# A one-core FFT and GEGLU kernel: the opening's gathers, first weights and early transforms put in another order, and later folds moved by some slots

## The chip, the cores and the metric

The kernel runs on one core of one Trainium2 chip. The metric is device microseconds of one execution. Each run below was timed beside runs of the kernel before on the same chip. The profiled span is about 1.8 us shorter than the time of the same execution, so spans are compared with spans and times with times.

The engines have the names of the profile: PE is TensorE (PEld its weight loads), DVE is VectorE, ACT is ScalarE, POOL is GpSimd, and SP is SyncE, whose queue issues transfers. An eviction is the copy by ACT or DVE of a matmul's result from a `ps_` tile to the tile where it is used.

## The reference

```python
def _attn_ref(x):                     # x: (8, 3008, 256) float32
    X = np.fft.fft(x, axis=1)
    X = np.fft.fft(X, axis=2)
    return X.real.astype(np.float32)

def _moe_ref(x, w_gate, w_val, w_out):   # 24064 tokens, d 256, d_ff 1536
    g = x @ w_gate
    gelu = 0.5 * g * (1.0 + erf(g * inv_sqrt2))
    val = x @ w_val
    return (gelu * val @ w_out).astype(np.float32)
```

The real part of a two-dimensional Fourier transform of each of eight batches goes through a gated feed-forward layer.

## The kernel before

The kernel splits each sequence into an even part E and an odd part O, by adding and subtracting x and its mirror image. The mirror comes by an indirect transfer with an index (a gather, issued by POOL). For one batch the steps are: fold (x and mirror to `eo_sb`), stage 1 (matmuls with `G`), an identity transform (`ch`, to `Z_sb`), twiddle transforms (`tp_e`, `tp_o`, `tp_y`, to `EO_sb` and `EB_sb`), and then the feed. The feed has 36 slots for each batch, 288 in all. A slot has the gate matmuls, two gelus on ACT (0.59 us each), the value matmuls, three DVE operations (0.66, 0.60 and 0.60 us from one start to the next), one product on POOL (1.15 us) and, from slot 12 on, two second-layer pieces of four matmuls (0.85 us together). `plan()` puts everything else into slots: transforms and loads as "fill", folds as "pool". The first transforms of batch 0 come before the feed, in `opening()`; all the others run hidden beside it.

The end of the opening:

```python
    def opening():
        # ... staging loads, constants, gathers, weight loads (see the diff)
        warm(9)                       # dummy matmuls; the number is how many
        vec_fills(); vec_consts(); g_phases()
        g_sin(9, 7); g_sin_ends(); g_sin(1, 8)
        t_columns()                   # ten tiny matmuls: "parity columns", L371
        t_phases(); t_sin()
        warm(15)
        cw_phases(); cw_sin()
        # ... gelu_table() is the load of ACT's gelu table, L395
        # ... folds and stage 1 of batch 0, piece by piece
        stage1(0)
        ch(0, 0)()
        ch(0, 1, "V")()               # "V": DVE evicts, otherwise ACT
        make_w(0, 0, 256, engine="V")()
        tp_e(0, 0)()
        tp_o(0, 0, "V")()
        make_w(1, 0, 256, engine="V")()
        tp_y(0, 0)()
        make_yw(0, 256)()
```

The parts of the plan that the change touches, and the load and the row copies:

```python
        for i, f in enumerate(early):          # batch 0, groups 1 and 2: ch, ch, tp_e, tp_o, tp_y
            at(fill, (3, 4, 5, 6, 6, 7, 8, 10, 11, 12)[i], f)
        # ...
        def spread(b, items, s0, s1):
            each = len(items) // NG
            for i, f in enumerate(items):
                s = s0 + i * (s1 - s0) // (len(items) - 1)
                at(fill, s, f)
                if i % each == each - 1:
                    at(fill, s + 1, tp_rows(b, i // each))
        # ...
        for b in range(2, B):
            s0 = (b - 1) * NS
            # ... ops: the folds of batch b
            first, n = (s0 - 13, 29) if b == 2 else (s0 - 22, 32)
            slot_of = [first + i * n // len(ops) for i in range(len(ops))]
            # ... folds into pool; loads of the batch after:
                    at(fill, slot_of[piece * per + 1] + 1, lambda b=b, k=k: load_part(b + 1, k))
            s = s0 - 9
            for i, (jg, piece) in enumerate(((2, 1), (1, 2), (0, 3), (3, 4))):
                ready = slot_of[piece * per + per - 1] + 1
                for g in range(2):
                    s = max(s + 1, ready)
                    at(fill, s, s1t(b, jg, g))
            # ... z_write, z_read, and the transforms by spread(b, items, s + 7, ...)

    def load_part(b, k):
        j0, nj = ((9, 8), (1, 8), (0, 1))[k]
        load_forward(b, j0, nj)       # plain load, SP's queue, L152
        load_mirror(b, j0, nj)        # gather, POOL's queue, L158

    def tp_rows(b, gi):               # one row of Z's transform, from DRAM
        def run():
            # 128 copies of the row to EB_sb (128 KB), L588, then once to EO_sb (1 KB), L590;
            # both on SP's queue
            nc.sync.dma_start(out=_sub(EB_bufs[b], ...), in_=...)
            nc.sync.dma_start(out=_sub(EO_bufs[b], ...), in_=...)
        return run
```

Of the kernel before, what the change touches and what calls it, by code (L numbers as in the profile page):

```python
# [28 lines left out]
def kernel(  # L29
# [69 lines left out]
    def stage_tile():  # L99
        return work([NPX, 9, C], FP32, "h", 2, "x_stage")  # L100
# [247 lines left out]
    def cw_sin():  # L348
        nc.scalar.activation(_sub(CW, [[256, 2], [1, 128]], 0), cd[:, :], AF.Sin, scale=-TWO_PI)
# [380 lines left out]
    def opening():  # L730
        stage[0] = stage_tile()
        xb[0] = xb_tile(0)
        for j0, nj, at in ((9, 8, 0), (0, 1, 8)):
            nc.sync.dma_start(
                out=_sub(stage[0], [[1, nj * C]], at * C),
                in_=ap_replace(x, ap=[[32 * C, NPX], [1, nj * C]], offset=x.offset + j0 * C))
        pool_consts()
        index_consts(0)
        cast_mirror(0, 9, 8)
        pool_consts2()  # L740
        index_consts(1)
        cast_mirror(0, 0, 1)
        cast_forward(0, 1, 8)
        cast_mirror(0, 5, 4)
        cast_mirror(0, 1, 4)
        for f0, n in ((0, 256), (256, 256), (512, 1024)):
            load_w(f0, n)
        for q in range(4):
            load_wo(q)
        idle = gelu_tile()[:, 0, :]  # L750
        nc.vector.memset(idle, 0.0)

        def warm(n):

            ps = psum("o")
            for _ in range(n):
                nc.tensor.matmul(ps[:, :], idle[:, 0:128], idle[:, :], start=True, stop=True)  # L757

        def fold_piece(j0, nj):
            for f in fold_ops(0, j0, nj, nc.vector):  # L760
                f()

        def stage1(jg):
            s1(0, jg, 0)()
            s1(0, jg, 1, "V" if jg == 0 else "A")()

        warm(9)
        vec_fills()
        vec_consts()
        g_phases()  # L770
        g_sin(9, 7)
        g_sin_ends()
        g_sin(1, 8)
        t_columns()
        t_phases()
        t_sin()
        warm(15)
        cw_phases()
        cw_sin()
        nc.vector.tensor_scalar(keep2, col_p, 1.0, None, op0=ALU.min)  # L780
        nc.vector.tensor_scalar(keep2, keep2, -2.0, None, op0=ALU.mult)
        gelu_table()
        t_write()
        identities()
        cw_rest()
        fold_piece(9, 4)
        stage1(2)
        warm(4)
        fold_piece(13, 4)
        fold_piece(0, 1)  # L790
        stage1(3)
        warm(5)
        fold_piece(5, 4)
        stage1(1)
        warm(3)
        fold_piece(3, 2)
        fold_piece(1, 2)
        stage1(0)
        ch(0, 0)()
        ch(0, 1, "V")()  # L800
        make_w(0, 0, 256, engine="V")()
        tp_e(0, 0)()
        tp_o(0, 0, "V")()
        make_w(1, 0, 256, engine="V")()
        tp_y(0, 0)()
        make_yw(0, 256)()

    NS = NG * NFC

    def plan():  # L810

        fill, pool = {}, {}

        def at(table, s, f):
            table.setdefault(s, []).append(f)

        early = []
        for gi in (1, 2):
            early += [ch(0, 2 * gi), ch(0, 2 * gi + 1, "V"), tp_e(0, gi), tp_o(0, gi, "V"), tp_y(0, gi)]
        for s, f in (  # L820
                (0, make_w(0, 256, 256)), (0, make_w(1, 256, 256)), (1, make_yw(256, 256)),
                (1, make_w(1, 512, 512, (1,))), (2, make_w(0, 512, 512, (0,))), (2, make_yw(512, 512)),
                (3, make_w(0, 512, 512, (1,))), (3, make_w(1, 512, 512, (0,))),
                (4, make_w(1, 1024, 512, (1,))), (5, make_w(0, 1024, 512, (0,))), (5, make_yw(1024, 512)),
                (6, make_w(0, 1024, 512, (1,))), (7, make_w(1, 1024, 512, (0,)))):
            at(fill, s, f)
        for i, f in enumerate(early):
            at(fill, (3, 4, 5, 6, 6, 7, 8, 10, 11, 12)[i], f)

        def second_x():  # L830
            xb[1] = xb_tile(1)
            cast_forward(1, 9, 8)

        for s, f in (
                (0, second_x), (1, lambda: cast_mirror(1, 9, 8)), (2, lambda: cast_forward(1, 0, 9)),
                (3, lambda: cast_mirror(1, 5, 4)), (4, lambda: cast_mirror(1, 1, 4)),
                (5, lambda: cast_mirror(1, 0, 1))):
            at(fill, s, f)
        ops = []
        for piece in PIECES:  # L840
            ops += fold_ops(1, *piece, nc.gpsimd)
        slot_of = [6 + i * 13 // len(ops) for i in range(len(ops))]
        for s, f in zip(slot_of, ops):
            at(pool, s, f)
        s = 10
        for jg, piece in ((2, 1), (1, 2), (0, 3), (3, 4)):
            for g in range(2):
                s = max(s + 1, slot_of[2 * piece + 1] + 1)
                at(fill, s, s1(1, jg, g))
        last1 = s  # L850
        for k, s in ((0, 18), (1, 19), (2, 19)):
            at(fill, s, lambda k=k: load_part(2, k))
# [10 lines that stand above are left out]
        items = []  # L863
        for gi in range(NG):
            items += [ch(1, 2 * gi), ch(1, 2 * gi + 1), tp_y(1, gi), tp_e(1, gi), tp_o(1, gi)]
        spread(1, items, last1 + 1, NS - 3)
        for b in range(2, B):
            s0 = (b - 1) * NS
            ops = []
            for j0, nj in PIECES:  # L870
                ops += fold_ops(b, j0, nj, nc.gpsimd)
            per = len(ops) // 5
            first, n = (s0 - 13, 29) if b == 2 else (s0 - 22, 32)
            slot_of = [first + i * n // len(ops) for i in range(len(ops))]
            for s, f in zip(slot_of, ops):
                at(pool, s, f)
            if b + 1 < B:
                for k, piece in ((0, 1), (1, 3), (2, 4)):
                    at(fill, slot_of[piece * per + 1] + 1, lambda b=b, k=k: load_part(b + 1, k))
            s = s0 - 9  # L880
            for i, (jg, piece) in enumerate(((2, 1), (1, 2), (0, 3), (3, 4))):
                ready = slot_of[piece * per + per - 1] + 1
                for g in range(2):
                    s = max(s + 1, ready)
                    at(fill, s, s1t(b, jg, g))
                if i == 2:
                    at(fill, s + 1, z_write(b, 0, 12))
                if i == 3:
                    at(fill, s + 1, z_write(b, 12, 4))
            at(fill, s + 3, z_read(b))  # L890
            items = []
            for gi in range(NG):
                items += [tp_y(b, gi), tp_e(b, gi), tp_o(b, gi)]
            assert s + 7 < s0 + NS - 10
            spread(b, items, s + 7, s0 + NS - 3)
        return fill, pool

    def feed():
        blocks, works = [], []
        for b in range(B):  # L900
            for parts, l2s in ffn_work(b):
                works.append(l2s)
                blocks += [(parts, fc) for fc in range(NFC)]
        fill, pool = plan()
        pend, before = [], None
        for i, (parts, fc) in enumerate(blocks):
            if fc == 0 and i:
                assert not pend
                pend = list(works[i // NFC - 1])
            parts["G"][fc]()  # L910
            if before:
                before[0]["g"][before[1]]()
            parts["V"][fc]()
            if pend:
                pend.pop(0)()
            for f in pool.pop(i, []):
                f()
            if before:
                before[0]["v"][before[1]]()
            if pend:  # L920
                pend.pop(0)()
            for f in fill.pop(i, []):
                f()
            before = parts, fc
        assert not fill and not pool
        before[0]["g"][before[1]]()
        before[0]["v"][before[1]]()
        for u in works[-1]:
            u()
# [33 lines left out]
```

## Time and profile before

| | before |
|---|---|
| time, median of 3 runs | 635.71 us (635.58 to 636.37) |
| profiled span | 633.9 us |
| TensorE busy | 620.3 us, 98% |
| first gate matmul starts | 22.70 us |
| first gelu of slot 0, of slot 12 | 23.35 us, 49.38 us |

The busy times of the engines, from the page of before (busy us, share of the span, number of instructions):

```profile
PE 620.3 (98%) x4289; PEld 409.6 (65%) x4289; DVE 582.4 (92%) x937; ACT 433.0 (68%) x855; POOL 505.8 (80%) x511
```

TensorE is close to full, but that is an average. The view of waits of before, for TensorE from 60 us to the end, has what TensorE waited for, then us in total, times, and the longest:

```profile
PE ps_dft L508 <- POOL eo_sb L224: 1.2, 1, 1.2
PE ps_o L695 <- POOL h_sb L671: 0.3, 1, 0.3
PE ps_dft L695 <- POOL h_sb L671: 0.3, 1, 0.3
```

So after 60 us only 1.8 us of waiting is left, 1.2 of it in one place, stage 1 of a batch that waits for POOL's fold. The chain of waits of before (start, us, what) puts that place at 124 us:

```profile
123.16 1.28 POOL eo_sb L224
```

Everything else that can be won is in the opening and in the slots without second-layer work. From the timeline of before (start us, us, engine, line, operation, count; in brackets the idle time before it and what ended that):

```profile
3.44 1.56 POOL L281 IOTA par<- 1x128 f32 x1
3.67 1.36 DVE L322 TENSOR_SCALAR ff<-ff 94x24 f32<-94x24 f32 x1
5.27 2.29 PE L371 MATMUL ps_v<-one,par 1*128 1x1 f32 x10
7.49 6.02 PE L757 MATMUL ps_o<-gelu_sb 128*128 128x512 bf16 x15
11.20 1.28 ACT L395 ACT_TABLE_LOAD   x1
15.38 0.47 ACT L473 ACTIVATE A_sb<-ps_g 128x384 bf16<-128x384 f32 x1
22.70 0.61 PE L622 MATMUL ps_g<-EO_sb,W_sb 128*128 128x512 bf16 x2
23.35 0.60 ACT L638 ACTIVATE gelu_sb<-ps_g 128x512 bf16<-128x512 f32 x1 [0.37 <-PE ps_g L622]
```

L371 are the parity columns, L757 the dummy matmuls that are meant to keep TensorE's clock up, L473 the copies of stage 1, L622 the gate. ACT's path to the gate runs from the table load at 11.20.

### The profile page before, as it was taken

The page shows a single profiled execution, that of the slowest core. Times are in us where ns is not written, and L with a number is a line of the kernel's source. Part 1 is how long each engine was busy: PE and PEld are TensorE (multiplying, and loading weights), DVE is VectorE, ACT ScalarE, POOL GpSimd, SP SyncE. Part 2 cuts the span into 40 slices and gives each one's busy share as a digit, 9 for nine tenths or more (in the row PEclk, how much of TensorE's full clock was granted, in tenths as well). Part 3 has the DMA queues.
Part 4 walks back from the last instruction along what each step waited for, and adds up shares of the span by engine and source line. Part 5 has one row for each costly group of instructions (what it writes and reads, how often), then busy time and mean ns, then how long its engine had stood idle before and what let it go on. Part 6 is the DMA issues. An engine that isn't in the chain of part 4 may idle for free.

```text
span 633.9 us, 13022 instructions
## 1 busy us (share of the span) xinstructions
PE 620.3 (98%) x4289; PEld 409.6 (65%) x4289; DVE 582.4 (92%) x937; ACT 433.0 (68%) x855; POOL 505.8 (80%) x511
## 2 busy tenths in 40 slices
PE   9889999999999999999999999999999999999997
PEld 4446666666666666666666666666666666666666
DVE  8689889899899999999999999999999999999992
ACT  5787777676766677666776667676777667666661
POOL 8489699989997899879998799968998555555551
PEclk9999999999999999999999999999999999999999
DMA  8940835534563353533636325633221332221123
GB/s 151 166 74 18 223 87 145 135 96 121 143 157 89 104 127 83 147 100 100 152 79 167 100 59 142 140 100 109 52 59 47 87 101 53 55 52 38 43 51 79
DMA packets 51993, 63.83 MB, mean 101 GB/s; under 512 B 7783, under 2 KB 47194, under 8 KB 49530
## 3 DMA queue, kind: packets, MB, share of 16 engines
q1 hardware_dynamic: 45238, 47.23, 29.0%
q0 software_dynamic: 6096, 15.29, 11.5%
q8 instruction: 33, 0.54, 0.4%
q10 hardware_dynamic: 592, 0.49, 0.3%
q14 instruction: 34, 0.28, 0.1%
HBM read 38.86 MB, written 29.38 MB: 108 GB/s over the span
## 4 chain that ended last, share of the span: by engine, by line
PE 85%; POOL 5%; ACT 5%; DVE 3%; issue 1%; POOLq 0%; ACTq 0%; DVEq 0%
PE ps_o L695 35%; PE ps_g L622 27%; PE ps_v L622 17%; POOL h_sb L671 3%; PE ps_dft L508 2%; PE ps_dft L544 2%; DVE v_sb L669 1%; ACT gelu_sb L638 1%; POOL eo_sb L224 1%; ACT gelu_sb L647 1%; PE ps_dft L489 1%; PE ps_dft L574 0%; DVE ve_sb L656 0%; ACT W_sb L423 0%; ACT A_sb L473 0%
## 5 line engine op out<-in xcount | busy, mean ns | idle before, releaser
L671 POOL TENSOR_TENSOR h_sb<-gelu_sb,v_sb 128x512 bf16<-128x512 bf16 (+1 forms) x288 | 328.8, 1145 | 107.8 <-DVE v_sb L669 93.2
L695 PE MATMUL ps_o<-Wo_sb,h_sb 128*128 128x256 bf16 (+1 forms) x2232 | 334.9, 273 | 0.3 <-POOL h_sb L671 0.3
L695 PEld LDWEIGHTS <-h_sb 128*128 128x128 bf16 (+1 forms) x2304 | 228.9, 100 | 111.7 <-POOL h_sb L671 2.0
L656 DVE SCALAR_TENSOR_TENSOR ve_sb<-EB_sb,yw,ps_v 128x512 f32<-128x512 bf16 (+1 forms) x288 | 212.3, 737 | 32.7 <-PE ps_v L622 30.8
L638 ACT ACTIVATE gelu_sb<-ps_g 128x512 bf16<-128x512 f32 (+1 forms) x288 | 169.5, 589 | 91.8 <-PE ps_g L622 91.5
L622 PE MATMUL ps_g<-EO_sb,W_sb 128*128 128x512 bf16 (+1 forms) x864 | 230.8, 376 | 1.5 <-ACT gelu_sb L647 1.4
L622 PE MATMUL ps_v<-EO_sb,W_sb 128*128 128x512 bf16 (+1 forms) x576 | 214.5, 376 | 0.0
L667 DVE TENSOR_TENSOR h_sb<-gelu_sb,ps_v 128x512 bf16<-128x512 bf16 (+1 forms) x288 | 195.2, 678 | 0.9 <-ACT gelu_sb L647 0.7
L669 DVE SCALAR_TENSOR_TENSOR v_sb<-ve_sb,ps_v 128x512 f32<-128x512 f32 (+1 forms) x288 | 192.8, 670 | 0.0
L622 PEld LDWEIGHTS <-W_sb 128*128 128x128 bf16 x1440 | 136.9, 98 | 79.1 <-issue 2.4
L647 ACT ACTIVATE gelu_sb<-ps_g 128x512 bf16<-128x512 f32 (+1 forms) x288 | 168.7, 586 | 0.0
L714 ACT ACTIVATE out_sb<-ps_o 128x512 f32<-128x512 f32 x92 | 54.9, 597 | 35.6 <-PE ps_o L695 35.1
L224 POOL TENSOR_TENSOR eo_sb<-ab_sb 94x512 bf16<-94x512 f32 (+1 forms) x60 | 66.6, 1110 | 0.1
L511 ACT ACTIVATE S_sb<-ps_dft 96x512 bf16<-96x512 f32 x48 | 28.2, 588 | 21.6 <-PE ps_dft L508 21.6
L554 ACT ACTIVATE EO_sb<-ps_dft 128x512 bf16<-128x512 f32 (+1 forms) x44 | 26.0, 590 | 22.4 <-PE ps_dft L544 22.4
L217 POOL TENSOR_TENSOR ab_sb<-x_raw,x_raw 94x508 f32<-94x508 f32 (+1 forms) x30 | 33.0, 1100 | 0.0
L220 POOL TENSOR_TENSOR ab_sb<-x_raw,x_raw 94x508 f32<-94x508 f32 (+1 forms) x30 | 32.9, 1097 | 0.0
L508 PE MATMUL ps_dft<-eo_sb,G 94*96 94x256 bf16 x102 | 19.2, 273 | 1.6 <-POOL eo_sb L224 1.2
L158 POOL DMA_INDIRECT x_raw<-in_x_dram,idx x18 | 17.0, 945 | 2.9 <-issue 1.5
L544 PE MATMUL ps_dft<-TP,Z_sb 128*128 128x128 bf16 (+1 forms) x188 | 18.0, 218 | 0.3 <-ACT W_sb L423 0.3
L544 PEld LDWEIGHTS <-Z_sb 128*128 128x128 bf16 x192 | 14.6, 98 | 2.6 <-DVE Z_sb L496 0.5
L757 PE MATMUL ps_o<-gelu_sb 128*128 128x512 bf16 x36 | 13.1, 529 | 1.2 <-DVE one L290 1.2
(128 smaller groups left out, 176.5 us busy)
## 6 DMA issues: line engine op xcount, KB each, us to landing
out_dram<-out_sb SPq DMA_DIRECT2D x361, 64.0 KB
x_raw<-in_x_dram SPq DMA_DIRECT2D x10, 768.0 KB
Z_sb<-z SPq DMA_DIRECT2D x6, 768.0 KB
z<-S_sb SPq DMA_DIRECT2D x6, 576.0 KB
EB_sb<-yrow SPq DMA_DIRECT2D x14, 128.0 KB
x_raw<-in_x_dram SPq DMA_DIRECT2D x2, 640.0 KB
z<-S_sb SPq DMA_DIRECT2D x6, 192.0 KB
EB_sb<-yrow SPq DMA_DIRECT2D x7, 120.2 KB
```

Source lines behind the costliest of these rows:

```text
L217: eng.tensor_tensor(ab(0, 1, up), fwd(1, up), mir(255, down), op=ALU.add)
L224: eng.tensor_tensor(_sub(eo, [[C, nj], [1, 128]], j0 * C + g * 128), ab(0, 0, [[1, 128]]), ab(1, 0, [[1, 128]]), op=op)
L544: nc.tensor.matmul(ps[:, o : o + n], st["Z"][:, pair, g * 128 : g * 128 + 128], _sub(TP, [[1, n]], g * 128), start=True, stop=True)
L622: nc.tensor.matmul(ps[:, :n], W[nm, part][:, fs], src, start=start, stop=stop, **kw)
L638: nc.scalar.activation(gl[:, 0, :n], pg[:, :n], AF.Gelu)
L647: nc.scalar.activation(_sub(gl, [[-1, n]], TOK + n - 1), pg[:, :n], AF.Gelu)
L656: nc.vector.scalar_tensor_tensor(ve[:, :n], EB_bufs[b][:, c0 : c0 + n], yw[:, fc : fc + 1], pv[:, :n], op0=ALU.mult, op1=ALU.add)
L667: nc.vector.tensor_tensor(st["h"][:, fc, 0, :n], gl[:, 0, :n], pv[:, :n], op=ALU.mult)
L669: nc.vector.scalar_tensor_tensor(_sub(vv, [[-1, n]], n - 1), ve[:, :n], 2.0, pv[:, :n], op0=ALU.mult, op1=ALU.subtract)
L671: nc.gpsimd.tensor_tensor(st["h"][:, fc, 1, :n], gl[:, 1, :n], vv[:, :n], op=ALU.mult)
L695: nc.tensor.matmul(pso[:m, half], st["h"][:, fc, sign, h0 : h0 + m], Wo_sb[:, fc, :], start=(fc == 0), stop=(fc == NFC - 1),)
L714: nc.scalar.activation(_sub(osb, [[1, 2 * C]], 0, part_num=m), pso[:m, :], AF.Copy)
```

## The change

The intent has four parts. (1) In the opening POOL makes the constants of the parity row before the first gather, so that the gathers follow one another ahead of the small constants of the last of them; DVE makes the phases of the matrix CW while TensorE turns the parity row. (2) The first weights are made before and between the identity transforms, during waits, and the first `yw` and `EB` are put behind the matmuls of the first gate. (3) The early transforms of batch 0 go one to a slot, 7 to 16, behind the weights. (4) The folds of batch 3 start three slots later (and end one slot later, for there are 30 slots for them instead of 32), and stage 1 of batches 1 to 7 follows its folds by two slots, no longer by one.

```diff
--- before.py
+++ after.py
@@ -735,14 +735,14 @@
                 out=_sub(stage[0], [[1, nj * C]], at * C),
                 in_=ap_replace(x, ap=[[32 * C, NPX], [1, nj * C]], offset=x.offset + j0 * C))
         pool_consts()
+        pool_consts2()
         index_consts(0)
         cast_mirror(0, 9, 8)
-        pool_consts2()
-        index_consts(1)
-        cast_mirror(0, 0, 1)
         cast_forward(0, 1, 8)
         cast_mirror(0, 5, 4)
         cast_mirror(0, 1, 4)
+        index_consts(1)
+        cast_mirror(0, 0, 1)
         for f0, n in ((0, 256), (256, 256), (512, 1024)):
             load_w(f0, n)
         for q in range(4):
@@ -764,19 +764,19 @@
             s1(0, jg, 0)()
             s1(0, jg, 1, "V" if jg == 0 else "A")()
 
-        warm(9)
-        vec_fills()
+        warm(11)
         vec_consts()
         g_phases()
+        vec_fills()
+        cw_phases()
         g_sin(9, 7)
         g_sin_ends()
         g_sin(1, 8)
+        cw_sin()
         t_columns()
         t_phases()
         t_sin()
-        warm(15)
-        cw_phases()
-        cw_sin()
+        warm(10)
         nc.vector.tensor_scalar(keep2, col_p, 1.0, None, op0=ALU.min)
         nc.vector.tensor_scalar(keep2, keep2, -2.0, None, op0=ALU.mult)
         gelu_table()
@@ -787,23 +787,26 @@
         stage1(2)
         warm(4)
         fold_piece(13, 4)
+        fold_piece(5, 4)
+        warm(2)
+        stage1(1)
+        warm(3)
         fold_piece(0, 1)
         stage1(3)
-        warm(5)
-        fold_piece(5, 4)
-        stage1(1)
-        warm(3)
+        warm(2)
         fold_piece(3, 2)
         fold_piece(1, 2)
         stage1(0)
+        make_w(0, 0, 256, engine="V")()
         ch(0, 0)()
         ch(0, 1, "V")()
-        make_w(0, 0, 256, engine="V")()
+        make_w(1, 0, 256, engine="V")()
         tp_e(0, 0)()
         tp_o(0, 0, "V")()
-        make_w(1, 0, 256, engine="V")()
+
+    def behind_first_gate():
+        make_yw(0, 256)()
         tp_y(0, 0)()
-        make_yw(0, 256)()
 
     NS = NG * NFC
 
@@ -825,7 +828,7 @@
                 (6, make_w(0, 1024, 512, (1,))), (7, make_w(1, 1024, 512, (0,)))):
             at(fill, s, f)
         for i, f in enumerate(early):
-            at(fill, (3, 4, 5, 6, 6, 7, 8, 10, 11, 12)[i], f)
+            at(fill, (7, 8, 9, 10, 11, 12, 13, 14, 15, 16)[i], f)
 
         def second_x():
             xb[1] = xb_tile(1)
@@ -842,10 +845,10 @@
         slot_of = [6 + i * 13 // len(ops) for i in range(len(ops))]
         for s, f in zip(slot_of, ops):
             at(pool, s, f)
-        s = 10
+        s = 12
         for jg, piece in ((2, 1), (1, 2), (0, 3), (3, 4)):
             for g in range(2):
-                s = max(s + 1, slot_of[2 * piece + 1] + 1)
+                s = max(s + 1, slot_of[2 * piece + 1] + 2)
                 at(fill, s, s1(1, jg, g))
         last1 = s
         for k, s in ((0, 18), (1, 19), (2, 19)):
@@ -870,7 +873,7 @@
             for j0, nj in PIECES:
                 ops += fold_ops(b, j0, nj, nc.gpsimd)
             per = len(ops) // 5
-            first, n = (s0 - 13, 29) if b == 2 else (s0 - 22, 32)
+            first, n = {2: (s0 - 13, 29), 3: (s0 - 19, 30)}.get(b, (s0 - 22, 32))
             slot_of = [first + i * n // len(ops) for i in range(len(ops))]
             for s, f in zip(slot_of, ops):
                 at(pool, s, f)
@@ -879,7 +882,7 @@
                     at(fill, slot_of[piece * per + 1] + 1, lambda b=b, k=k: load_part(b + 1, k))
             s = s0 - 9
             for i, (jg, piece) in enumerate(((2, 1), (1, 2), (0, 3), (3, 4))):
-                ready = slot_of[piece * per + per - 1] + 1
+                ready = slot_of[piece * per + per - 1] + 2
                 for g in range(2):
                     s = max(s + 1, ready)
                     at(fill, s, s1t(b, jg, g))
@@ -908,6 +911,8 @@
                 assert not pend
                 pend = list(works[i // NFC - 1])
             parts["G"][fc]()
+            if i == 0:
+                behind_first_gate()
             if before:
                 before[0]["g"][before[1]]()
             parts["V"][fc]()
```

## The prediction

> **What bounds the kernel.** The page gives TensorE busy 98% of 633.9 us. After 60 us the view of waits shows three TensorE waits only: 1.2 us at 124 us (for POOL's fold), 0.3 and 0.3. All 288 slots keep their matmuls. What the change can reach is the first 60 us:
>
> - Opening: the first gate matmul starts at 22.7 us (timeline). ACT leads to it: gelu table load at 11.20 (1.28 us) behind DVE's twiddle, then CW phases; constants to 15.4; seven stage 1 copies without a gap, 15.38 to 18.14; identity transforms at 18.19.
> - Slots 0 to 11, without second-layer work: gates from 22.7 to 48.7, 26.0 us. DVE needs 0.66+0.60+0.60 = 1.86 us a slot (start to start), 12 slots 22.3, plus evictions; it idles about 3.4 us, chiefly while ACT carries gelus (1.1 us a slot), weight evictions (0.5 to 0.6 each) and early transforms at once.
>
> **What the change does.**
>
> 1. Constants. The parity row comes before the first gather (2.27 us before, now estimate 3 to 4.5); the other gathers go earlier (8.93 and 10.21, now estimate 6 to 8), weight loads about 1 us earlier (11.13). DVE makes CW's phases while TensorE turns parity rows (2.3 us), so they leave the path between twiddle sine and table load. Expected: table load near 10.4, ACT's stage 1 copies near 14.6. POOL and DVE hinder each other there: a 24-element DVE operation took 1.36 us beside the 1.56 us iota. The Trainium skill, "SBUF — State Buffer", section "SBUF: two separate sides", calls this an exclusive lock on a shared port pair; the trace agrees in kind. So part may be lost. Gain 0.7 us (-0.4 to 1.0).
> 2. First weights before the identity transforms; first yw and EB after the first gate's matmuls. Before, 1.05 us pass from the last EO eviction (21.65) to the gate. Gain about 1.2 us, some given back as yw and EB now delay the first value operation. First gate predicted near 20.8 us.
> 3. Early transforms one a slot, 7 to 16. ACT in slots 3 to 8 loses three 0.6 us evictions; TensorE's waits for ACT (0.8, 0.7, 0.3, and 0.7 in slot 12) mostly go. Slots 0 to 11 become DVE-bound: 22.3+1.2, with idling 24.6 instead of 26.0. But five transforms, 1.7 us of TensorE, move into slots 12 to 16, already full (second layer 0.85 us, first 1.07), less 0.9 that slots 12 and 13 lose. Net 0.6 us (-0.5 to 1.5).
> 4. Batch 3's folds start three slots later; stage 1 follows folds one slot later: the wait at 124 us should vanish, the 0.3 at 83 us perhaps. Gain 1.0 us.
>
> Sum 0.7+1.2+0.6+1.0 = 3.5. From slot 20 on, slots keep their length.
>
> **Predicted: 632.2 us, range 630.4 to 634.4.** Faster by over 2%: 0.01; within 2%: 0.985; slower by over 2%: 0.005.
>
> **Right if:** first gate at 20 to 21.5 us; table load before 11 us; gates 0 to 12 apart by 24 to 25.3 us; DVE nearly gapless from slot 3; slots 12 to 16 about 2.4 us each; no TensorE wait for POOL's fold near 120 us; slots of the second half unchanged (about 2.1 us).
>
> **Wrong if:** POOL's constants, blocked by DVE, make the gathers or weights late; fills after G's phases delay the parity columns and the table load; weights for slots 1 to 4 have not landed when the feed comes 2 us earlier (DMA is full up to 38 us); later fold slots make new waits.

## More of the kernel before

The view by windows of before, for one stretch of the opening and for slots 4 to 12 and 12 to 16 (length, busy us and instructions of each engine, granted clock, DMA share, GB/s):

```profile
4.00:8.00 4.00, 3.94 (x15) 2.59 (x14) 2.94 (x5) 1.27 (x4) 3.50 (x9) 1.00 0.79 166
32.34:49.38 17.04, 14.71 (x98) 7.87 (x97) 15.92 (x26) 13.77 (x28) 15.34 (x17) 1.00 0.38 62
49.38:58.83 9.45, 8.79 (x70) 5.85 (x69) 9.15 (x15) 6.77 (x13) 9.24 (x11) 1.00 0.05 12
```

In slots 4 to 12 DVE (the third busy time, 15.92 of 17.04 us) is the fullest engine.

Last, a place that looks harmless in before, around slot 99, from its timeline (SPq is the queue of SP, POOL L158 a gather, ACT L554 an eviction of a twiddle transform into `EO_sb`):

```profile
225.01 0.52 SPq L588 DMA_DIRECT2D EB_sb<-yrow  x1
225.63 0.25 SPq L590 DMA_DIRECT2D EO_sb<-yrow  x1
230.92 0.93 POOL L158 DMA_INDIRECT x_raw<-in_x_dram,idx  x1
231.78 0.33 SPq L152 DMA_DIRECT2D x_raw<-in_x_dram  x1
236.31 0.60 ACT L554 ACTIVATE EO_sb<-ps_dft 128x512 bf16<-128x512 f32 x1 [0.62 <-PE ps_dft L544]
```

The row copies are issued at 225 us, the gather almost 6 us later, and the eviction at 236.31 waits for TensorE only.

## The result, and the profile after

| | before | after |
|---|---|---|
| time, median | 635.75 us of 4 runs (635.58 to 636.37) | 633.61 us of 4 runs (633.44 to 633.91) |
| ratio | | 0.9965, 95% interval 0.9948 to 0.9982 |
| profiled span | 633.9 us | 632.1 us |
| first gate matmul | 22.70 us | 20.47 us |

A ratio here is the mean time of one kernel's fast runs over that of the other's fast runs of the same rounds, so it is not quite the ratio of the medians quoted. For the experiments below the ratios come out when the profiled run is left out. The change gains 2.1 us by the medians; 3.5 were summed up, 632.2 predicted. The time lies in the range.

The busy times of after:

```profile
PE 618.9 (98%) x4285; PEld 407.4 (64%) x4285; DVE 580.9 (92%) x937; ACT 432.7 (68%) x855; POOL 505.7 (80%) x511
```

The view of TensorE's waits of after, from 60 us on:

```profile
PE ps_g L622 <- ACT gelu_sb L647: 1.0, 2, 0.8
PE ps_dft L574 <- DMA Z_sb<-z: 0.5, 2, 0.2
PE ps_o L695 <- POOL h_sb L671: 0.3, 1, 0.3
PE ps_dft L695 <- POOL h_sb L671: 0.3, 1, 0.3
```

The wait for the fold is gone, and other waits have come: their sum is 2.1 us where it was 1.8. The opening in the timeline of after:

```profile
1.51 1.38 POOL L281 IOTA par<- 1x128 f32 x1
2.38 0.72 DVE L321 TENSOR_SCALAR ff<-ff 94x384 f32<-94x384 f32 x1
4.26 1.68 POOL L158 DMA_INDIRECT xb<-in_x_dram,idx  x1 [0.29 <-POOL idx L268]
5.58 1.27 PE L371 MATMUL ps_v<-one,par 1*128 1x1 f32 x10
9.24 1.28 ACT L395 ACT_TABLE_LOAD   x1
10.02 0.19 DVE L216 TENSOR_TENSOR eo_sb<-x_stage,xb 94x8 bf16<-94x8 f32 x1 [0.89 <-DMA xb<-in_x_dram,idx]
10.84 0.34 PE L467 MATMUL ps_g<-G,eo_sb 94*128 94x96 bf16 x4 [1.72 <-DVE eo_sb L217]
11.62 2.67 PE L757 MATMUL ps_o<-gelu_sb 128*128 128x512 bf16 x6
14.65 0.49 ACT L473 ACTIVATE A_sb<-ps_dft 128x384 bf16<-128x384 f32 x1 [0.38 <-PE ps_dft L467]
16.10 0.49 ACT L473 ACTIVATE A_sb<-ps_v 128x384 bf16<-128x384 f32 x1 [0.58 <-PE ps_v L467]
20.47 0.38 PE L622 MATMUL ps_g<-EO_sb,W_sb 128*128 128x512 bf16 x1
```

The table load comes 2.0 us earlier, but the folds now wait for the gather (0.89 us at 10.02), TensorE waits 1.72 us for the folds, and the copies of stage 1 on ACT, without a gap in before, wait twice. The view by windows of after, for the stretch of the opening behind that wait and for slots 4 to 12 and 12 to 16:

```profile
12.00:16.00 4.00, 3.94 (x25) 1.90 (x23) 3.02 (x14) 3.11 (x12) 4.00 (x6) 0.58 1.09 143
30.39:45.86 15.47, 13.81 (x77) 6.60 (x78) 14.80 (x24) 12.73 (x26) 14.52 (x16) 1.00 0.47 78
45.86:56.71 10.85, 10.22 (x86) 6.93 (x85) 9.85 (x17) 7.15 (x14) 10.85 (x12) 1.00 0.07 18
```

TensorE's granted clock falls after its idle time: 0.58 is the mean of the window, and the clock records in the packed trace say half speed from 11.94 to 15.35 us. Slots 4 to 12 take 15.5 us instead of 17.0, slots 12 to 16 take 10.9 instead of 9.5. And around slot 99, in the timeline of after:

```profile
228.00 0.94 POOL L158 DMA_INDIRECT x_raw<-in_x_dram,idx  x1
228.62 0.35 SPq L588 DMA_DIRECT2D EB_sb<-yrow  x1
229.08 0.23 SPq L590 DMA_DIRECT2D EO_sb<-yrow  x1
229.41 0.32 SPq L152 DMA_DIRECT2D x_raw<-in_x_dram  x1
234.79 0.60 ACT L554 ACTIVATE EO_sb<-ps_dft 128x512 bf16<-128x512 f32 x1 [1.59 <-PE ps_o L695]
```

The gather is now issued just before the row copies, and ACT's eviction waits 1.59 us. The view names a second-layer matmul as what ended that wait. This eviction has no use for that matmul; the control run below names the copy itself.

The best single measure of where time comes and goes is the start of the first gelu of a slot, read from the trace. The first row has the times of before in us, the others the difference to it (minus is earlier); the labels are those of the experiments:

```
slot           0      1      4      8     12     16     20     28     44     48     64     68     96    100    287
before     23.35  25.32  32.34  42.02  49.38  58.83  67.44  86.29 119.91 129.53 162.10 171.17 228.71 236.81 616.79
after      -1.82  -1.13  -1.95  -3.97  -3.52  -2.12  -1.95  -1.75  -1.83  -2.92  -2.73  -2.48  -3.01  -1.52  -1.84
e12_after  -1.96  -1.27  -2.03  -4.05  -3.60  -2.21  -2.05  -0.88  -0.96  -2.05  -2.19  -1.66  -2.20  -0.96  -1.49
e1_load98  -1.83  -1.14  -1.95  -3.97  -3.53  -2.10  -1.93  -1.05  -1.13  -2.22  -2.36  -1.60  -2.13  -1.91  -2.24
e2_later   -0.91  -0.91  -0.91  -0.91  -0.91  -0.92  -0.92  -0.71  -0.80  -1.89  -1.91  -1.52  -2.04  -0.72  -0.83
e3_fold3   -0.92  -0.92  -0.92  -0.92  -0.92  -0.92  -0.92  -0.40  -0.41  -0.41  -0.43  +0.22  +1.49  +1.49  +1.49
e5_warm11  -0.97  -0.97  -0.97  -0.97  -0.97  -0.97  -0.98  -0.70  -0.70  -0.70  -0.69  -0.69  -0.69  -0.68  -0.71
e9_consts  -0.80  -0.80  -0.80  -0.80  -0.80  -0.80  -0.80  -0.95  -0.95  -0.95  -0.98  -0.57  -0.56  -0.55  -0.55
e10_weights -1.23 -0.54  -0.54  -0.54  -0.54  -0.54  -0.54  -0.76  -0.76  -0.76  -0.79  +0.10  +0.10  +0.11  +0.11
e4_open    -1.74  -1.05  -1.05  -1.05  -1.05  -1.05  -1.05  -1.24  -1.24  -1.24  -1.26  +0.03  +0.04  +0.04  +0.02
e8_oldearly -1.68 -0.99  -0.33  -0.33  -0.39  -0.94  -0.99  -0.68  -0.76  -1.85  -1.98  -1.60  -2.13  -1.06  -1.78
e11_best   -2.73  -2.04  -2.65  -4.67  -4.22  -2.81  -2.64  -2.93  -3.14  -4.46  -2.98  -3.10  -3.43  -3.21  -3.23
```

The row of after reads: 1.82 us won at the first gate, 0.69 of it given back at slot 1, much won up to slot 8 and more than half of that given back up to slot 16, 1.09 won between slots 44 and 48 (the fold wait), and 1.49 lost between slots 96 and 100. After slot 100 only 0.3 us moves.

### The profile page after: what moved, and what is told of

It reads as the page before. It is cut to its first block, busy times and chain, and to the rows that moved or that the text cites. A ratio compares the mean times of both kernels' runs of the same rounds, so it can differ in the third digit from the quotient of the medians.

```text
span 632.1 us, 13032 instructions
## 1 busy us (share of the span) xinstructions
PE 618.9 (98%) x4285; PEld 407.4 (64%) x4285; DVE 580.9 (92%) x937; ACT 432.7 (68%) x855; POOL 505.7 (80%) x511
## 4 chain that ended last, share of the span: by engine, by line
PE 87%; DMA 4%; DVE 3%; POOL 2%; ACT 2%; issue 1%; POOLq 0%; DVEq 0%; ACTq 0%
PE ps_o L695 36%; PE ps_g L622 27%; PE ps_v L622 17%; DMA Z_sb<-z 3%; PE ps_dft L508 2%; PE ps_dft L544 2%; POOL h_sb L671 1%; DVE v_sb L669 1%; DMA xb<-in_x_dram,idx 1%; DVE h_sb L667 1%; PE ps_o L757 1%; PE ps_dft L574 1%; ACT gelu_sb L638 1%; DVE ve_sb L656 1%; PE ps_g L695 0%
## 5 line engine op out<-in xcount | busy, mean ns | idle before, releaser
L757 PE MATMUL ps_o<-gelu_sb 128*128 128x512 bf16 x32 | 11.1, 498 | 1.2 <-DVE col L305 1.2
```

## The experiments

My theory: three of the four items worked, but item 4 moved batch 3's row copies into the slot where the first load of batch 5 is issued, and the late row copy costs what the fold wait had cost; and part of the 1.8 us at the first gate is no work of the change but a different state of TensorE's clock in the opening. The rival for the first point: whatever reaches slot 99 earlier runs into transfers whose landing does not move, so that the opening's gain, and not the slots, made the wait. The rival for the second: the change earned the whole 1.8 us.

### e12_after: the control

The kernel after, once more, in a later session.

> The changed kernel again, as a control beside the other three: 633.2 to 634.0 us as at first, columns of parity 1.27 us (early clock), and the wait of about 1.1 us at slot 99 again, if it belongs to the program and not to chance.

Measured: 633.81 us (633.09 to 634.27, 5 runs) against 635.56 of before; ratio 0.9968 (0.9955 to 0.9981). The result repeats. In the timeline of this run the eviction at slot 99 reads:

```profile
235.36 0.60 ACT L554 ACTIVATE EO_sb<-ps_dft 128x512 bf16<-128x512 f32 x1 [1.34 <-DMA EO_sb<-yrow]
```

Here the releaser is the 1 KB row copy by name, with 1.24 us lost between slots 96 and 100. What varies between two runs of the same kernel is seen as well: between slots 20 and 28 this run loses 1.17 us where the first one lost 0.20, to a wait for POOL's product that is 1.3 us long here and 0.3 there.

### e1_load98: the first load of batch 5 three slots later

```diff
-                    at(fill, slot_of[piece * per + 1] + 1, lambda b=b, k=k: load_part(b + 1, k))
+                    at(fill, slot_of[piece * per + 1] + 1 + (3 if (b, k) == (4, 0) else 0),
+                       lambda b=b, k=k: load_part(b + 1, k))
```

(an edit of after)

> The changed kernel, but the first x load of batch 5 three slots later (slot 98 instead of 95). Theory: after the change TensorE loses about 1.1 us near 235 us, because ScalarE's write of EO columns (slot 99) waits for the small copy of a row into the same EO buffer, and that copy was issued 0.3 us before two loads of 768 KB and landed only 5.7 us later. Moving the load takes that wait away: near 632.5 us, 1.0 to 1.2 us under the changed kernel's 633.6, ratio to the kernel before 0.995. Rival: the wait is for something else (gelu buffers, the second layer), the load's neighbourhood is chance; then 633.6 as before.

Measured: 632.73 us (631.82 to 633.53, 6 runs) against 635.79; ratio 0.9951 (0.9938 to 0.9964). This interval overlaps those of after and e12_after, so the times alone do not tell the kernels apart; the traces do. The loss between slots 96 and 100 fell from 1.49 to 0.22 us. From its timeline:

```profile
229.96 0.23 SPq L590 DMA_DIRECT2D EO_sb<-yrow  x1
234.41 0.60 ACT L554 ACTIVATE EO_sb<-ps_dft 128x512 bf16<-128x512 f32 x1 [0.33 <-PE ps_dft L544]
235.18 0.53 SPq L152 DMA_DIRECT2D x_raw<-in_x_dram  x1
```

With the load behind the eviction, the eviction waits for TensorE alone, though it comes as early as in after. So the wait came from the copy beside the load, and the opening's gain does not make it by itself. The DMA packets that started in each us, counted from the records of after, show how:

```
us of after's span               227  228  229  230  231  232  233  234
queue 0 (gather), 8192 B           0    0   12   11   32   27   13    1
queue 1 (SP), 1024 B             120   87   42    8   35   27   44   15
queue 1 (SP), 8192 B (load)        0    0    0    0    0    0   13   28
```

In 231 and 232 the 1 KB packets of SP's queue (row copies, and output stores behind them) take turns, one for one, with the gather's 8192-byte packets; the plain load's packets start when these are done. In before no packet of queue 0 started between 225 and 231 us, and the same copies, issued at 225.01 and 225.63, were through before 228 us. The Trainium skill, "DMA: Bandwidth & Descriptors", section "Queues, rings and completion order", says that each DMA engine goes round the queues it has work for and changes at packet boundaries; the counts agree in kind. What the page doesn't tell is the price: the 1 KB copy, issued at 229.08, was waited for until 234.8 us, 5.7 us. No run moved the gather without the plain load, so it is the packets, and no experiment, that point to the gather.

### e2_later: item 4 alone

```diff
-            first, n = (s0 - 13, 29) if b == 2 else (s0 - 22, 32)
+            first, n = {2: (s0 - 13, 29), 3: (s0 - 19, 30)}.get(b, (s0 - 22, 32))
-                ready = slot_of[piece * per + per - 1] + 1
+                ready = slot_of[piece * per + per - 1] + 2
```

(an edit of before; the diff also moves stage 1 of batch 1 by up to two slots, and that is left out here)

> The kernel before with only the later slots of the change: batch 3's folds three slots later, first-stage matmuls of batches 2 to 7 one slot later after a fold. Theory: TensorE's 1.2 us wait for the fold near 124 us is gone (slot 46 earlier by 1.2 to 1.5 us), but the new wait near slot 99 gives about 1.1 back: 635.4 to 635.8 us against 635.75. Rival (the later slots are a plain gain and the loss at slot 99 belongs to the opening): 634.3 to 634.7.

Measured: 635.1 us (633.21 to 635.35) against 635.79; ratio 0.9984 (0.9969 to 1.0). From its timeline:

```profile
5.28 1.27 PE L371 MATMUL ps_v<-one,par 1*128 1x1 f32 x10 [0.26 <-POOL par L284]
6.48 3.41 PE L757 MATMUL ps_o<-gelu_sb 128*128 128x512 bf16 x15
235.60 0.60 ACT L554 ACTIVATE EO_sb<-ps_dft 128x512 bf16<-128x512 f32 x1 [1.43 <-DMA EO_sb<-yrow]
```

The wait at slot 99 is there with the old opening: 1.32 us between slots 96 and 100. The fold wait is gone: 1.09 us between 44 and 48. From slot 44 to slot 287 item 4 is worth 0.03 us, nothing. The rival is out: the new wait belongs to the new slots.

This run brought the second finding. Its opening is that of before, yet its first gelu comes 0.91 us earlier. The ten parity columns take 1.27 us instead of 2.29, the fifteen dummies 3.41 instead of 6.02. That is 0.40 us for a matmul of 512 columns in before's profile and 0.23 here: TensorE ran at about half its speed for most of that stretch in the profiled execution of before. The view by windows gives a clock of 1.00 for 4 to 8 us of before, but the packed trace has no clock record there and the view counts that as full speed. The first record, of full speed, is at 12.80 us in before, and at 4.69 us here, 4.97 in e3 and 5.11 in after: records and durations agree.

### e3_fold3: the folds of batch 3 later, without the +2

```diff
-            first, n = (s0 - 13, 29) if b == 2 else (s0 - 22, 32)
+            first, n = {2: (s0 - 13, 29), 3: (s0 - 19, 30)}.get(b, (s0 - 22, 32))
```

(an edit of before)

> The kernel before with batch 3's folds three slots later and nothing else. The first row copy of batch 3 then stays or moves with the fold; if the new wait of slot 99 comes from the one-slot-later rule it is absent here, and the fold's wait near 124 us may be there in part, since the stage then starts one slot after the fold. Theory: 634.3 to 635.0 us. Rival (the fold shift alone makes the wait at slot 99): 635.4 to 635.8.

Measured: 637.5 us (636.88 to 638.29) against 635.79; ratio 1.0032 (1.0019 to 1.0046): 0.3% slower, a clear miss. Its view of TensorE's waits from 60 us on:

```profile
PE ps_dft L508 <- POOL eo_sb L224: 2.9, 3, 1.2
```

The first of the three, 1.19 us at 124 us, is that of before: it is stage 1 of batch 2, whose folds this edit does not touch. The other two are batch 3's own, 0.49 us at 164 us and 1.19 us at 190 us, where stage 1 now follows the later folds by one slot only. There is no wait at slot 99. So the later folds need the +2. The converse was not tried: by the arithmetic of `plan()` batch 3's first row copies stay at slot 94 with the three slots alone (this run) and would stay there with the +2 alone; only the two together put them at slot 95, beside the load. The +2 alone may thus have had the gain without the collision.

### e5_warm11: two more dummies before the parity columns

```diff
-        warm(9)
+        warm(11)
```

(an edit of before)

> The kernel before with 11 instead of 9 warm-up matmuls ahead of the parity columns, nothing else. Theory: part of the change's gain is TensorE's clock. In the profile of before all warm-up matmuls up to 12.6 us start 427 ns apart and the parity columns take 2.29 us; in two later profiles of the same opening they take 1.27 us and the first gelu comes at 22.43 instead of 23.35 us. With 11 matmuls the clock should have come up before the parity columns in every run: columns 1.27 us, first gelu near 22.5 us, mean time 0.3 to 0.9 us under before. Rival (two more matmuls only delay the columns by 0.85 us): first gelu 23.4 to 24.2, time same or up to 0.8 us longer.

Measured: 634.98 us (634.57 to 635.85, 5 runs) against 635.41; ratio 0.9996 (0.9983 to 1.001), not resolved. The profiled execution has the fast clock, with the columns in 1.27 us and the first gelu at 22.38. The Trainium skill, "TensorE: Matmul & The Clock Gate", section "What's actually happening", says that the clock comes up after about 3.4 us of sustained work in a window that runs freely, so that the same kernel measures different numbers of slow matmuls from run to run. The traces agree in kind: among the four profiles with nine dummies (before, e2, e3, e10) two have slow columns, and among the ten with eleven (after and e1, e4 to e9, e11, e12) only e6 has. The first record of full speed comes 2.9 to 4.5 us after the first dummy in the eleven others, and 11.6 to 12.9 us after it in these three; why it is so late there no run shows. Fourteen profiles don't settle whether the two dummies help.

### e9_consts: item 1 alone

The first two hunks of the diff's opening and the new order of the folds, on before (warm counts too), with the weights as before:

```diff
         pool_consts()
+        pool_consts2()
         index_consts(0)
...
-        warm(9)
-        vec_fills()
+        warm(11)
         vec_consts()
         g_phases()
+        vec_fills()
+        cw_phases()
...
```

> The kernel before with the change's constants, gather order and warm-up alone; first weights, yw and EB stay in their old place, all slots as before. Theory: table load at 9.24 us as in the whole change, ScalarE's stage 1 copies end 0.7 us earlier than in before (17.4 against 18.14), since the folds on DVE and a fallen clock now set their end; first gelu near 22.3 to 22.7 us against 23.35 in the profile of before (22.4 where its clock came up early): the constants give 0.7 to 1.0 us against a before with a late clock and nothing against one with an early clock. Time 635.0 to 635.6. Rival (the constants carry the whole gain of the gate): first gelu 21.5 to 21.8.

Measured: 635.17 us (634.59 to 635.62, 4 runs) against 635.56; ratio 0.9994 (0.9979 to 1.0008). In its profile the table load is at 9.24, as in after, and the first gelu comes 0.80 us earlier than in the profile of before. Beside an execution with before's opening at the fast clock (e2, 0.91; e3, 0.92) that is no gain, rather 0.1 us of loss. Table load and constants come earlier, but the folds wait for the gather, TensorE waits for the folds and its clock falls again, as the lines of after showed.

### e10_weights: item 2 alone

```diff
         stage1(0)
+        make_w(0, 0, 256, engine="V")()
         ch(0, 0)()
         ch(0, 1, "V")()
-        make_w(0, 0, 256, engine="V")()
+        make_w(1, 0, 256, engine="V")()
         tp_e(0, 0)()
         tp_o(0, 0, "V")()
-        make_w(1, 0, 256, engine="V")()
-        tp_y(0, 0)()
+    def behind_first_gate():
         make_yw(0, 256)()
+        tp_y(0, 0)()
```

(an edit of before, with the call of `behind_first_gate` in the feed as in the diff)

> The kernel before with only the second item of the change: first weights ahead of the identity transforms, yw and EB behind the first gate. Theory: first gelu 0.9 to 1.3 us earlier than with the same opening in before: about 21.4 with an early clock, 22.3 with a late one; 0.6 to 0.8 us of it given back at the second gelu. Rival (the first weights are not there yet so early, and the gate waits for DMA): no gain.

Measured: 635.62 us (634.97 to 635.8, 4 runs) against 635.56; ratio 0.9998 (0.9983 to 1.0012). The profile has the slow columns, as before's has, so the two compare directly: 1.23 us at the first gelu, 0.69 given back at slot 1, because `EB` and `yw` now delay the first value operation, and 0.54 kept. Then, between slots 64 and 68, it loses 0.89 us to a row copy, and ends where before does.

### e4_open: the whole opening, items 1 and 2

The opening of after with the plan of before.

```diff
         pool_consts()
+        pool_consts2()
...
         stage1(0)
+        make_w(0, 0, 256, engine="V")()
...
+    def behind_first_gate():
...
```

> The kernel before with only the opening of the change (constants, order of gathers, first weights, warm matmuls, yw and EB behind the first gate); early transforms and all later slots as before. Theory: first gelu 1.8 us earlier (21.5 us) as in the changed kernel; of that 1.1 to 1.8 us last to slot 12, since EB and yw give 0.7 back at slot 1 and the slots 3 to 8 still hang on ScalarE; the 1.2 us wait for the fold near 122 us is still there, and no wait at slot 99: 634.0 to 634.7 us. Rival (slots 0 to 11 absorb the earlier start, because weights or DMA set their pace): 635.2 or more.

Measured: 635.48 us (634.27 to 636.42) against 635.79; ratio 0.9993 (0.9978 to 1.0008): a miss. The first gelu is 1.74 us earlier, 1.05 us remain at slot 1, and 1.26 at slot 64. Then they are lost at once. From its timeline:

```profile
166.38 0.60 ACT L554 ACTIVATE EO_sb<-ps_dft 128x512 bf16<-128x512 f32 x1 [1.18 <-DMA EO_sb<-yrow]
```

Here the mechanism of the rival named at the head of this section is real, though near slot 66 and not at slot 99: the row copies of batch 2 are issued at 161.34 and 161.96 us, with a load and a gather of batch 4, issued at 156.41 and 155.70, still running. The load's 8192-byte packets are on the same queue ahead of the copies, and alternate with the gather's until 164 us. In before the load and the gather were issued about 1 us later and drained at about the same time. The landing did not move, so an earlier feed only waits for it longer. It need not be so: e5, with the same plan and 0.69 us ahead of before at slot 64, loses nothing there. In its trace the load's packets were through at 161 us, before most of the gather's, and the 1 KB packets began at 163.1 us, against 164.0 in before. So the opening's gain was lost in this profile, and no run shows that the old plan always loses it.

### e8_oldearly: after without item 3

```diff
-            at(fill, (7, 8, 9, 10, 11, 12, 13, 14, 15, 16)[i], f)
+            at(fill, (3, 4, 5, 6, 6, 7, 8, 10, 11, 12)[i], f)
```

(an edit of after)

> The changed kernel with the early transforms in their old slots (3 to 12). Theory: this part of the change is worth 0.9 us at slot 24 (from the profile of the opening alone: 1.05 us gained there, 1.96 in the whole change): slots 3 to 8 wait for ScalarE again as before, slot 12 near 48.3 us, slot 24 near 76.0 instead of 75.1; time 634.2 to 634.8 us if nothing later differs. Rival (what slots 12 to 16 give back eats it): 633.4 to 633.8, as the changed kernel.

Measured: 633.84 us (633.3 to 634.19, 5 runs) against 635.41; ratio 0.9973 (0.9959 to 0.9986). At slot 20 it is 0.99 us ahead of before, and after is 1.95: item 3 is worth 0.96 us there. At slot 287 the two stand at -1.78 and -1.84: almost all of it is gone: 0.32 us between slots 48 and 64, 0.42 between 96 and 100 (the wait at slot 99 costs 1.49 us in after and 1.07 here) and 0.40 behind slot 100, which I did not trace further. The time that I expected was 634.2 or more, so it missed. In the view of TensorE's waits of this run from 21 to 60 us there is one that before has not:

```profile
PE ps_dft L417 <- DMA w_raw<-in_moe_w_val_dram: 1.0, 1, 1.0
```

It is no work of the old slots: e4 has the same opening, the same slots and the same issue times of the weights, and no such wait, and e12_after, with the new slots, has one of 0.4 us. The landing of these weights varies from run to run. (Item 3 alone on before could not be tried: that build deadlocked in the simulator.)

### e6_load98_warm18: e1 with more dummies in the gap

```diff
-        warm(10)
+        warm(18)
```

(an edit of e1, meant to fill TensorE's idle time before the folds)

> The changed kernel with the load of batch 5 at slot 98, and 18 instead of 10 warm-up matmuls behind the parity columns, so that TensorE isn't idle from 9.1 to 10.8 us. Theory: in the changed kernel the clock falls back there (0.57 to 0.58 from 12 to 16 us, 427 ns matmuls), stage 1 is late by it and ScalarE waits 0.4 to 1.0 us for it. With TensorE kept busy the clock stays: first gelu 20.6 to 21.2 instead of 21.5 us, time 0.3 to 0.9 us under that of the changed kernel with the load moved (632.7): 631.8 to 632.4. Rival (the folds on DVE set the pace, the clock does not matter): first gelu 21.4 to 21.6, time as there.

Measured: 631.74 us median against 635.41; ratio 0.9942 (0.9928 to 0.9955, the profiled run left out). Five of the six runs lie between 631.42 and 632.24 us; the sixth took 636.86, and that is the one that was profiled. In its timeline the columns are slow:

```profile
6.00 2.29 PE L371 MATMUL ps_v<-one,par 1*128 1x1 f32 x10
```

The eighteen dummies took 6.92 us, most of them at the slow clock, and held up stage 1. The five other runs have no trace. What the dummies do when the clock is up is seen in the profile of e11, which has them too: no fall of the clock is recorded there, and its first gelu comes 0.90 us before that of e1. All seven profiles with the change's constants, ten dummies behind fast columns, have the fall. So the theory holds at the gate; what the dummies are worth in time is not told from e1, whose interval (0.9938 to 0.9964) overlaps and which ran on another chip.

### e7_load98_A: e1 with all early evictions on ACT

```diff
-            early += [ch(0, 2 * gi), ch(0, 2 * gi + 1, "V"), tp_e(0, gi), tp_o(0, gi, "V"), tp_y(0, gi)]
+            early += [ch(0, 2 * gi), ch(0, 2 * gi + 1), tp_e(0, gi), tp_o(0, gi), tp_y(0, gi)]
```

> The changed kernel with the load of batch 5 at slot 98, and all early transforms evicted by ScalarE instead of every other one by DVE. Theory: slots 8 to 11 are bound by DVE (1.86 us of gates and products a slot plus 0.6 us for an eviction in slots 8 and 10), while ScalarE idles 0.7 us a slot; so slot 12 comes 0.6 to 1.2 us earlier (gelu of slot 12 at 44.7 to 45.3 instead of 45.85 us), and slot 14 needs no wait for POOL behind a DVE eviction; kept to the end: 631.5 to 632.2 us. Rival (TensorE waits for ScalarE instead): 632.7 or more.

Measured: 634.43 us (633.93 to 634.96, 5 runs) against 635.41; ratio 0.9984 (0.997 to 0.9998): a miss. At slot 12 it was 0.55 us ahead of e1, and at slot 287 still 0.33. But its end took 18.7 us from the last slot's first gelu, where the others need about 17.2. In its timeline:

```profile
628.68 0.38 ACT L710 ACTIVATE out_sb<-ps_g 128x256 f32<-128x256 f32 x1 [3.29 <-DMA out_dram<-out_sb]
```

An output eviction waited 3.29 us for an earlier output's transfer. Why that transfer was late in this kernel is open.

### e11_best: the waits taken away one by one

After with the load of e1, the first load of batch 4 nine slots later, the folds of batch 2 one slot later, and 18 dummies:

```diff
-            first, n = {2: (s0 - 13, 29), 3: (s0 - 19, 30)}.get(b, (s0 - 22, 32))
+            first, n = {2: (s0 - 12, 28), 3: (s0 - 19, 30)}.get(b, (s0 - 22, 32))
-                    at(fill, slot_of[piece * per + 1] + 1, lambda b=b, k=k: load_part(b + 1, k))
+                    at(fill, slot_of[piece * per + 1] + 1 + {(4, 0): 3, (3, 0): 9}.get((b, k), 0),
+                       lambda b=b, k=k: load_part(b + 1, k))
```

> The changed kernel with four mends: first load of batch 5 at slot 98, first load of batch 4 at slot 70 instead of 61, batch 2's folds one slot later, 18 instead of 10 warm-up matmuls behind the parity columns. Theory: the waits at slots 27 (0.3 to 1.0 us, second layer for POOL), 66 (0.3 to 0.5 us, row copy behind a load) and 99 (1.1 us) are all gone, and the clock stays up in most runs: 630.5 to 631.5 us. Rival (with the early transforms full of slack, later waits for DMA swallow what is gained): 631.7 or more, as with the load and the warm-up alone.

Measured: 632.44 us (630.78 to 633.77, 6 runs) against 635.56; ratio 0.9946 (0.9931 to 0.9961). It beats before, and its median is 1.4 us under that of after on the same chip (e12_after, 633.81), though the two intervals just overlap; e6 has a lower median yet, on another chip and with one slow run, and the two are not told apart. I expected 630.5 to 631.5, and it missed. The losses around slots 28 and 66 are gone, the one at slot 99 is down to 0.22 us, and at slot 48 it is 4.46 us ahead of before. By slot 64 it has lost 1.48 of them again, in its timeline here:

```profile
151.90 0.22 PE L574 MATMUL ps_dft<-TP,Z_sb 128*4 128x128 bf16 x1 [1.43 <-DMA Z_sb<-z]
```

TensorE waits for the read of Z from DRAM. Here it is not a landing that stayed where it was while the feed came earlier: the read was issued earlier too, at 145.88 us against 148.01 in e1, but was waited for 6.0 us later, while in e1 it was there in 4.5. In e6, whose feed came later than that of e1, TensorE waits for it as well:

```profile
156.00 0.22 PE L574 MATMUL ps_dft<-TP,Z_sb 128*4 128x128 bf16 x1 [1.64 <-DMA Z_sb<-z]
```

Why the read took longer in these two is open.

## Why the prediction was right or wrong

The time, 633.61 us, lies in the range, and "within 2%" was right. The sum was too high, 3.5 us against 2.1 measured. By terms:

| term | predicted | measured | read from |
|---|---|---|---|
| 1 constants | 0.7 (-0.4 to 1.0) | about -0.1 | first gelu of e9 against e2, both at the fast clock |
| 2 first weights | 1.2, some given back | 1.23 at the gate, 0.54 kept | e10 against before, both at the slow clock |
| 2 behind item 1 | | 0.94 at the gate, 0.25 kept | e4 against e9, both at the fast clock |
| 3 early transforms | 0.6 (-0.5 to 1.5) | 0.9 | slot 20, after against e4 and e8 |
| 4 later folds | 1.0 | 0.0 | slot 44 to 287, after and e2 |

**The step that failed is the fourth term, "Gain 1.0 us".** The wait at 124 us did vanish, as I wrote, and with 1.1 us (slots 44 to 48). The risk "later fold slots make new waits" was on my list, but I put no number to it. The runs show it: the three slots and the +2 together moved batch 3's first row copies from slot 94 to slot 95, where the first load of batch 5 stands; the 1 KB copy took turns with the gather's packets, an eviction waited for it, and 1.1 to 1.5 us were lost (e8, e12, e2, after). With that load three slots later (e1) the stretch from slot 44 to 287 gains 1.11 us, which is the term as predicted. So its mechanism and size were right, and the collision took all of it. Since the wait at 124 us is batch 2's, the +2 is what took it away; the three slots for batch 3 alone left it as it was (e3).

**First gate: right in time, in part by luck.** I predicted 20.8 us, and it started at 20.47. (Its second matmul waited for DVE's eviction of `EO_sb` until 21.11 us, so that the gate moved by 2.23 us and the first gelu by 1.82.) But 0.9 of the 1.8 us between the two profiles at the first gelu is the state of TensorE's clock: executions with before's own opening come 0.91 and 0.92 us earlier too (e2, e3). I read 6.02 us for 15 dummies and did not divide. The table load moved further than predicted (9.24 against "near 10.4"), and so did the start of stage 1's copies (13.42 against 14.6); but at the fast clock the opening of before has them at 10.03 and 14.20 us already (e2). What was left gained nothing, for those copies then waited for the folds, and these for the gather. I predicted the gather's issue correctly (4.26 in "3 to 4.5") and did not follow it to its landing. The contention of POOL and DVE that I warned of moved with the constants: a DVE operation of 384 columns took 0.72 us beside the iota, and 0.36 in before. This agrees in kind with the exclusive lock that the prediction cites from the Trainium skill, "SBUF — State Buffer", section "SBUF: two separate sides".

**Second term: right at the gate, and half of it does not stay.** I wrote that some is given back and did not subtract it: 0.69 us at slot 1, in e4 and e10 and after alike.

**Third term: right at slot 20, its parts both too small, and not kept.** At slot 287 after is only 0.06 us ahead of e8. Slots 0 to 12 took 24.34 us (predicted 24.6; before 26.03), the 0.69 us of the second term included. DVE is busy 14.80 of 15.47 us in slots 4 to 12, 96% after 93%, so "nearly gapless" holds. But slots 12 to 16 took 2.71 us each, not 2.4 (before 2.36), and gave back 1.4 us where 1.7 less 0.9 was reckoned.

**The second half:** right. From slot 100 to slot 287 the difference moves by 0.3 us.

At the fast clock the terms as measured sum to about 1.0 us (-0.1, 0.25, 0.9 and 0.0). The trace of after beside that of e2, both at the fast clock, says the same: 1.03 us at slot 20, 1.01 at slot 287. The medians say 2.1. The missing 1.1 is about the size of the step between the two clock states of the opening (0.9), of which before's runs had an unknown mix (its times over all sessions go from 634.4 to 636.5 us); that this is the rest was not shown. Nor do terms simply add: e4 kept nothing of items 1 and 2 by the end, e8 nearly all that after has without item 3. What is won upstream can be lost at the next transfer whose landing has not moved (e4, e10), and need not be (e5).

## What to carry to other kernels

In a full kernel a gain upstream can be lost at any later transfer that something waits for and that does not land earlier too: before summing, list the small copies that are waited for, and see which large transfer each is issued beside or behind. When slots are shifted, check the other work in the slot it arrives at, for a copy that was harmless by itself can be late in company. When two shifts are made together, try each alone. Compare the durations of identical instructions in two profiles before giving a difference to the change: dummies of the same shape that take 0.40 us in one and 0.23 in the other say that the clocks differed.

## What the Trainium skill lacked or had wrong

- "TensorE: Matmul & The Clock Gate", section "What's actually happening": the run-to-run change of the clock's start that it describes is confirmed (columns 1.27 or 2.29 us for the same kernel's opening). It tells the reader that the ramp costs under 1% of a span. That holds here (0.9 us of 634 at the first gelu; 3.0 us, 0.5%, in the profile of e6 against that of e11, which has the same 18 dummies and fast columns), but it is as large as a whole tuning step; the page lacks the advice to sort runs by it.
- The same page, section "Seeing it yourself", warns that the trace's clock events can't be fully trusted. No run here shows it: in before the first record of full speed is at 12.80 us, and the dummies start 0.42 to 0.43 us apart until 12.6 us, and 0.22 after that where they follow one another directly; in after the record of half speed from 11.94 to 15.35 us fits them too. What misled me is that none of the fourteen traces has a record before the clock first comes up (4.05 to 14.05 us), which the page does not say, and that the view by windows counts this as 1.00.
- "DMA: Bandwidth & Descriptors", section "Queues, rings and completion order", has the turn-taking by packets, but not its price for a small copy: 5.7 us from the issue of a 1 KB copy to the end of the wait for it, beside a gather of 8192-byte packets.
- No page I read has the time of an iota on POOL into one partition: 1.38 to 1.56 us for 128 elements with a four-level pattern, against 0.23 us for a plain one over 128 partitions. DVE was at work beside it in both profiles, so what it takes alone is not shown.
